# Two pools for the small tiles, and the start of every large SBUF tile moved to a multiple of 512 bytes

## The chip, the cores and the metric

The kernel runs on one core of a Trainium2 chip. The metric is the device time of one launch in microseconds. Three runs of the kernel before gave 735.39, 735.44 and 735.93 us, a median of 735.44 us.

## What is computed

Cut from the reference: an attention in both directions between `x` (8 batches, 8 heads, 512 tokens, depth 64) and `state` (32 rows for each head), and then a gated feed-forward layer on the 8 x (512 + 32) tokens of 512 numbers each.

```python
scores = scale * x @ state.T          # softmax over the 32 state rows
xread  = softmax(scores) @ state
scores2 = scale * state @ x.T         # softmax over the 512 tokens
sread  = softmax(scores2) @ x
x = concat([xread, sread]) as (4608 tokens, 512)
a = x @ w_a; b = x @ w_b              # 512 -> 1536
out = (a * b) @ w_out                 # 1536 -> 512
```

## The kernel before, in words

The 64-bit weights are split into a high and a low float32r part, and each product of the feed-forward layer is made of three TensorE matmuls (high by high, high by low, low by high).

The work goes by visits: a unit (one of the 8 batches, or `States`, the 256 state rows of all batches together) and a list of chunks of the 1536 hidden columns. Twelve column tiles `ft` of 128 make up the 1536. For each unit and `ft` there is a `layer1` and a `layer2`:

- `layer1` (batch): twelve 512-column matmuls into two PSUM banks `ab`. The weights loaded into TensorE (`lhsT`) are slices of `p_h` and `p_l`, the moving operand (`rhs`) is `at_h` or `at_l`.
- `layer2` (batch): twelve 512-column matmuls into four PSUM banks `acc`. The weights are slices of `g_h` and `g_l`, the moving operand is a half of a tile `wo0` to `wo11`.
- `layer1` of `States`: twenty-four 256-column matmuls, with weights from `wq` or `sw_st` and `x_nat` (high) or `x_raw` (low) as the moving operand.
- `project`: products of the states with the first weights, in pairs into a bank `ms` (the first ones into `acc`), with weights `sd_h`, `sd_l` and `wq` as the moving operand.

In every one of them each matmul has its own weight load. The three parts repeat in the order high-high, high-low, low-high.

All instructions are recorded first; then `plan` puts them in an order for each engine by costs and due times that are written in the kernel, and this order is issued as it stands (all of it from line 1047, which is why the profile shows that line alone). `plan` knows shapes, pool names as keys and numbers of buffers; it knows no addresses. All DMAs are issued from one queue (SP).

The small tiles are `m1` (three times 16 floats, 192 bytes in each partition, 2 buffers) and `m2` (4 floats, 16 bytes, 8 buffers of 32 bytes each with the padding); both hold the maxima and sums of the softmaxes. Before, both are tiles of the pool `att`.

The pools lie in SBUF one behind the other in the order in which they are opened. In the program of the kernel before, the first free byte of a partition is 16512, which is 128 more than a multiple of 512. The places that follow from it:

| tiles | first byte in the partition | remainder by 512 |
|---|---|---|
| `ident` (const0), `xst` (const) | 16512, 17024 | 128 |
| all of `proj`: `raw`, `t1`, `t2`, `wq`, `sd_h`, `sd_l`, `sw_st`, `wo0` to `wo11` | 21120 to 127616 | 128 |
| `x_raw` (first of att) | 127616 | 128 |
| `m1`, 2 buffers | 132224 | (small) |
| `s_p`, `x_nat`, `at_h`, `at_l` (att) | 132608 to 165376 | 0 |
| `m2`, 8 buffers | 165376 | (small) |
| `e2`, `a2`, `a_tr` (att) | 165632 to 171776 | 256 |
| all of `mlp`: `stg`, `p_raw`, `p_h`, `p_l`, `a_sb`, `g_h`, `g_l` | 171776 to 229120 | 256 |

Each large tile has a size that is a multiple of 512 bytes, and so has each slice that a 512-column matmul reads (128 columns of weights are 512 bytes, 512 columns are 2048).

Of the kernel before, what the change touches and what calls it, by code (L numbers as in the profile page):

```python
# [10 lines left out]
F32 = mybir.dt.float32  # L11
# [9 lines left out]
P = 128  # L21
# [393 lines left out]
def attn_moe(ctx, tc, xt, xn, sd, wl, w_out, out):  # L415
# [9 lines left out]
    def pool(name, bufs, free=False, **kw):  # L425
        p = Pool(ctx.enter_context(tc.tile_pool(name=name, bufs=bufs, **kw)), name, bufs, free)
        pools.append(p)
        return p

    const0 = ctx.enter_context(tc.tile_pool(name="const0", bufs=1))  # L430
    const = pool("const", 1)
    proj = pool("proj", 2)
    att = pool("att", 2)
    mlp = pool("mlp", 2)
    dram = pool("dram", 1, space=bass.MemoryType.DRAM)
    ps_acc = pool("ps_acc", 4, space=bass.MemoryType.PSUM)
    ps_ab = pool("ps_ab", 2, space=bass.MemoryType.PSUM)
# [5 lines left out]
    def minus(eng, out, in0, in1):  # L443
        eng.tensor_tensor(out=out, in0=in0, in1=in1, op=ALU.subtract)
# [149 lines left out]
    class Attention:  # L594
# [37 lines left out]

        def soft_t(self):

            m1 = self.m1 = att.tile([P, 3, 16], F32, name="m1")
            sp = self.sp
            t = self.t.rearrange("p (a b) -> p a b", b=32)
            nc.vector.tensor_reduce(out=m1[:, 0, :], in_=t, axis=AX.X, op=ALU.max)
            minus(nc.vector, sp, t, m1[:, 0, :].unsqueeze(2).broadcast_to([P, 16, 32]))
# [9 lines left out]

        def soft(self):  # L650

            m2 = self.m2 = att.tile([P, 4], F32, name="m2", bufs=8)
            nc.vector.tensor_reduce(out=m2[:, 0:1], in_=self.s, axis=AX.X, op=ALU.max)
            nc.vector.tensor_scalar_mul(out=m2[:, 1:2], in0=m2[:, 0:1], scalar1=-SCALE)
            if self.b not in WIDE:
                self.turn()
            nc.scalar.activation(out=self.e2, in_=self.s, func=AF.Exp, bias=m2[:, 1:2], scale=SCALE,
                                 accum_out=m2[:, 2:3])

        def turn(self):  # L660
            sp = self.sp
            nc.vector.transpose(out=sp.rearrange("p a b -> p (a b)"), in_=self.s)

            m1 = self.m1 = att.tile([P, 3, 16], F32, name="m1")
            nc.vector.tensor_reduce(out=m1[:, 0, :], in_=sp, axis=AX.X, op=ALU.max)
            minus(nc.vector, sp, sp, m1[:, 0, :].unsqueeze(2).broadcast_to([P, 16, 32]))

# [422 lines left out]
```

## Time and profile before

| | us |
|---|---|
| median of three runs | 735.44 |
| the profiled execution, its own time | 734.27 |
| its span, first to last instruction | 732.5 |
| TensorE matmuls busy | 706.2 |
| VectorE (DVE) busy | 495.8 |
| ScalarE (ACT) busy | 394.9 |

The span is the time from the first to the last instruction of the program; 1.8 us of the execution's time lie outside it. "PE" is TensorE's matmuls and "PEld" its weight loads, which overlap them. A matmul's own duration in the profile (about 0.4 us) is longer than the time from its start to the start of the next one, since matmuls are pipelined; what a row of matmuls costs is therefore read from starts, or from the chain of work that ended last, where each piece counts only the time that it adds.

### The profile page before, as it was taken

To read this page: it belongs to the slowest core of one execution; us is meant where nothing else is said; L and a number is where in the kernel's file an instruction comes from. 1 tells how busy PE (TensorE), PEld (TensorE's weight loads), DVE (VectorE), ACT (ScalarE), POOL (GpSimd) and SP (SyncE) were. 2 spreads that over 40 slices of the span, in tenths; PEclk is the share of its full clock that TensorE was granted. 3 is DMA by queue.
4 is the path that set the end of the run, shared out by engine and by line. 5 is a ranking of instruction groups with operands and counts; after the bars stand their busy time and mean duration, and the time that the engine had idled before them with its cause. 6 is when DMAs were issued, how large, how long until landed. Compare 5 with 4: busy or idle time off the path is not lost.

```text
span 732.5 us, 9629 instructions
## 1 busy us (share of the span) xinstructions
PE 706.2 (96%) x3440; PEld 557.7 (76%) x3440; DVE 495.8 (68%) x947; ACT 394.9 (54%) x723; POOL 0.7 (0%) x6
## 2 busy tenths in 40 slices
PE   5898899998999999999999999999999999999997
PEld 4565657785887888788888887886788888988886
DVE  5986795995847967684799548637879833795322
ACT  4966785686846459786445325234456433553222
POOL 0000000000000000000000000000000000000000
PEclk9999999999999999999999999999999999999999
DMA  9667867677788436859988133324425311501002
GB/s 339 219 225 276 278 238 241 240 278 268 259 286 309 158 142 243 272 193 354 356 314 288 38 115 123 115 64 134 159 57 198 119 58 30 199 31 30 1 0 87
DMA packets 55087, 134.32 MB, mean 183 GB/s; under 512 B 5632, under 2 KB 5632, under 8 KB 55040
## 3 DMA queue, kind: packets, MB, share of 16 engines
q1 hardware_dynamic: 55040, 133.71, 52.5%
q8 instruction: 27, 0.44, 0.3%
q14 instruction: 20, 0.16, 0.1%
HBM read 87.03 MB, written 46.66 MB: 183 GB/s over the span
## 4 chain that ended last, share of the span: by engine, by line
PE 92%; ACT 5%; DMA 1%; DVE 1%; issue 1%; DVEq 0%; SPq 0%; ACTq 0%
PE ab L1047 40%; PE acc L1047 39%; PE ms L1047 13%; ACT wq L1047 2%; DMA p_raw<-scr 1%; DMA x_raw<-xt 0%; ACT stg L1047 0%; ACT t L1047 0%; ACT wo L1047 0%; ACT p_h L1047 0%; ACT sd_h L1047 0%; ACT e L1047 0%; DVE m L1047 0%; ACT sw_st L1047 0%; ACT at_h L1047 0%
## 5 line engine op out<-in xcount | busy, mean ns | idle before, releaser
L1047 PE MATMUL acc<-wo,g_h 128*128 128x512 f32 x816 | 259.3, 397 | 0.1
L1047 PEld LDWEIGHTS acc<-wo,g_h 128*128 128x128 f32 x816 | 151.4, 188 | 37.0 <-issue 2.3
L1047 DVE TENSOR_TENSOR a_sb<-ab,a_sb 128x512 f32<-128x512 f32 (+1 forms) x108 | 71.3, 661 | 138.9 <-PE ab L1047 131.8
L1047 PE MATMUL acc<-wo,g_l 128*128 128x512 f32 x408 | 159.3, 396 | 0.0
L1047 PE MATMUL ab<-at_h,p_h 128*128 128x512 f32 x384 | 152.4, 400 | 1.9 <-ACT p_h L1047 1.7
L1047 PE MATMUL ab<-at_l,p_h 128*128 128x512 f32 x384 | 152.2, 397 | 0.0
L1047 PE MATMUL ab<-at_h,p_l 128*128 128x512 f32 x384 | 150.8, 396 | 0.0
L1047 ACT COPY a_sb<-ab 128x512 f32<-128x512 f32 (+1 forms) x108 | 60.9, 564 | 150.7 <-PE ab L1047 149.6
L1047 ACT CAST g_h<-a_sb 128x512 fp32r<-128x512 f32 (+1 forms) x108 | 64.6, 598 | 53.2 <-DVE a_sb L1047 52.9
L1047 PEld LDWEIGHTS acc<-wo,g_l 128*128 128x128 f32 x408 | 76.5, 188 | 18.3 <-issue 1.0
L1047 PEld LDWEIGHTS ab<-at_h,p_h 128*128 128x128 f32 x384 | 73.0, 190 | 22.4 <-ACT p_h L1047 3.6
L1047 PEld LDWEIGHTS ab<-at_h,p_l 128*128 128x128 f32 x384 | 72.7, 189 | 20.1 <-issue 3.1
L1047 PEld LDWEIGHTS ab<-at_l,p_h 128*128 128x128 f32 x384 | 72.9, 190 | 17.0 <-issue 1.8
L1047 DVE TENSOR_TENSOR g_l<-a_sb,g_h 128x512 fp32r<-128x512 f32 (+1 forms) x108 | 70.8, 655 | 20.9 <-ACT g_h L1047 20.8
L1047 DVE TENSOR_TENSOR p_l<-p_raw,p_h 128x512 fp32r<-128x512 f32 x92 | 60.0, 684 | 11.7 <-ACT p_h L1047 11.7
L1047 ACT CAST p_h<-p_raw 128x512 fp32r<-128x512 f32 x92 | 52.8, 619 | 13.8 <-PE ab L1047 9.3
L1047 DVE TENSOR_SCALAR t<-t 128x512 int32<-128x512 int32 x120 | 49.8, 422 | 9.6 <-ACT t L1047 8.5
L1047 PE MATMUL ms<-wq,sd_h 128*128 128x512 f32 (+2 forms) x112 | 38.8, 418 | 7.3 <-ACT wo L1047 3.9
L1047 ACT CAST wq<-t 64x512 fp32r<-64x512 f32 (+1 forms) x64 | 39.4, 619 | 8.2 <-PE ms L1047 2.9
L1047 DVE SCALAR_TENSOR_TENSOR t<-raw,t 128x512 int32<-128x512 int32 (+1 forms) x60 | 39.7, 686 | 0.3
L1047 PE MATMUL ms<-wq,sd_l 128*128 128x512 f32 (+2 forms) x112 | 37.7, 406 | 0.0
L1047 ACT COPY wo<-ms 128x512 f32<-128x512 f32 x44 | 25.8, 590 | 12.8 <-PE ms L1047 11.5
(93 smaller groups left out, 702.2 us busy)
## 6 DMA issues: line engine op xcount, KB each, us to landing
p_raw<-scr SPq DMA_DIRECT2D x46, 512.0 KB, 4.4
scr<-sw_st SPq DMA_DIRECT2D x48, 256.0 KB, 4.2
scr<-wo SPq DMA_DIRECT2D x48, 256.0 KB, 4.2
raw<-wl SPq DMA_DIRECT2D x22, 512.0 KB, 5.8
part<-stg SPq DMA_DIRECT2D x20, 512.0 KB, 3.0
stg<-part SPq DMA_DIRECT2D x20, 512.0 KB, 6.1
out<-stg SPq DMA_DIRECT2D x34, 256.0 KB, 2.4
x_raw<-xt SPq DMA_DIRECT2D x14, 576.0 KB, 3.9
```

The costliest lines, as they stand in the source:

```text
L1047: getattr(obj, method)(*map(real, args), **{k: real(x) for k, x in kw.items()})
```

## The change

A pool `small` is opened ahead of all others and holds the two buffers of `m1` (384 bytes), and a pool `tail` is opened behind `mlp` and holds the eight buffers of `m2` (256 bytes). No instruction is added, removed or given another shape, and no tile has another number of buffers.

```diff
+    small = pool("small", 2)
     const0 = ctx.enter_context(tc.tile_pool(name="const0", bufs=1))
     const = pool("const", 1)
     proj = pool("proj", 2)
     att = pool("att", 2)
     mlp = pool("mlp", 2)
+    tail = pool("tail", 8)
...
-            m1 = self.m1 = att.tile([P, 3, 16], F32, name="m1")
+            m1 = self.m1 = small.tile([P, 3, 16], F32, name="m1")
...
-            m2 = self.m2 = att.tile([P, 4], F32, name="m2", bufs=8)
+            m2 = self.m2 = tail.tile([P, 4], F32, name="m2")
...
-            m1 = self.m1 = att.tile([P, 3, 16], F32, name="m1")
+            m1 = self.m1 = small.tile([P, 3, 16], F32, name="m1")
```

The places follow from the sizes: 16512 + 384 = 16896 = 33 x 512, so `ident`, `xst`, all of `proj` and `x_raw` move up by 384 bytes to remainder 0; `s_p` to `at_l` stay where they were; `e2`, `a2`, `a_tr` and all of `mlp` move down by 256 bytes, also to remainder 0.

## Rows read from the trace of the kernel before

**Rows 1.** The page: busy time of each engine, granted clock, DMA share in 40 slices.
```profile
PE 706.2 (96%) x3440; PEld 557.7 (76%) x3440; DVE 495.8 (68%) x947; ACT 394.9 (54%) x723; POOL 0.7 (0%) x6
...
PEclk9999999999999999999999999999999999999999
DMA  9667867677788436859988133324425311501002
```

**Rows 2.** The page: the chain that ended last, by engine, as shares of the span.
```profile
PE 92%; ACT 5%; DMA 1%; DVE 1%; issue 1%; DVEq 0%; SPq 0%; ACTq 0%
```

**Rows 3.** Groups of matmuls by shape: count, busy us and mean ns, idle before.
```profile
L1047 PE MATMUL acc<-wo,g_h 128*128 128x512 f32 x816 | 259.3, 397 | 0.1
L1047 PE MATMUL acc<-wo,g_l 128*128 128x512 f32 x408 | 159.3, 396 | 0.0
L1047 PE MATMUL ab<-at_h,p_h 128*128 128x512 f32 x384 | 152.4, 400 | 1.9 <-ACT p_h L1047 1.7
...
L1047 PE MATMUL ms<-wq,sd_h 128*128 128x512 f32 x80 | 31.9, 399 | 3.1 <-ACT wo L1047 2.4 <-ACT sw_st L1047 0.8
```

**Rows 4.** The chain in order of time: start us, us added, engine and tile.
```profile
211.40 2.77 PE ab L1047 x12
...
267.12 0.93 PE ms L1047 x4
...
376.76 2.73 PE ab L1047 x12
379.50 2.79 PE acc L1047 x12
...
628.46 2.83 PE ab L1047 x24
...
700.53 2.73 PE ab L1047 x12
703.26 2.79 PE acc L1047 x12
```

**Rows 5.** TensorE's timeline, 203.1 to 204.5 us: start, duration, operation.
```profile
203.36 0.39 PE L1047 MATMUL ms<-wq,sd_h 128*128 128x512 f32 x1
203.59 0.39 PE L1047 MATMUL ms<-wq,sd_l 128*128 128x512 f32 x1
203.82 0.39 PE L1047 MATMUL ms<-wq,sd_h 128*128 128x512 f32 x1
204.04 0.40 PE L1047 MATMUL ms<-wq,sd_l 128*128 128x512 f32 x1
204.28 0.39 PE L1047 MATMUL ab<-at_l,p_h 128*128 128x512 f32 x1
```

**Rows 6.** Groups by shape again: DVE and ACT on tiles of different remainders, `States` matmuls.
```profile
L1047 DVE TENSOR_TENSOR p_l<-p_raw,p_h 128x512 fp32r<-128x512 f32 x92 | 60.0, 684 | 11.7 <-ACT p_h L1047 11.7
...
L1047 ACT CAST p_h<-p_raw 128x512 fp32r<-128x512 f32 x92 | 52.8, 619 | 13.8 <-PE ab L1047 9.3 <-DMA p_raw<-scr 4.3
...
L1047 DVE SCALAR_TENSOR_TENSOR t<-raw,t 128x512 int32<-128x512 int32 x30 | 20.6, 686 | 0.2
...
L1047 ACT CAST wq<-t 128x512 fp32r<-128x512 f32 x16 | 9.9, 622 | 2.6 <-PE ab L1047 2.0 <-DVE t L1047 0.6
...
L1047 DVE TENSOR_TENSOR at_l<-a_tr,at_h 128x512 fp32r<-128x512 f32 x12 | 8.2, 683 | 0.0
...
L1047 ACT CAST at_h<-a_tr 128x512 fp32r<-128x512 f32 x12 | 7.5, 621 | 5.4 <-DVE a_tr L1047 5.4
```

**Rows 7.** TensorE's busy time on `acc` in two stretches: length, busy (count), clock, DMA share, GB/s.
```profile
0.00:200.00 200.00, 64.55 (x274) 0.99 0.74 262
200.00:732.50 532.50, 257.84 (x1020) 1.00 0.45 154
```

**Rows 8.** DMA issues: source and target, count, KB each, median us to landing.
```profile
scr<-sw_st SPq DMA_DIRECT2D x48, 256.0 KB, 4.2
```

**Rows 9.** TensorE's waits: who waited for whom, us in total, times, longest.
```profile
PE ms L1047 <- DMA x_raw<-xt: 4.3, 1, 4.3
```

## The prediction

> **What bounds the kernel now.** I read the page first. [...] Next come the matmuls by shape: 1224 `acc` matmuls of `layer2` (816 + 408), 1152 `ab` matmuls of `layer1` (three groups of 384, of which one stands), and 160 `ms` matmuls of `project` (two groups of 80, one stands) [rows 3]. The mean ns there is no cost, because matmuls overlap; all of these groups show 396 to 400.
>
> The cost is in the chain in order of time. In the regular stretches (about 345 to 437, 565 to 622 and 650 to 705 us) it alternates between twelve `ab` matmuls in 2.73 us and twelve `acc` matmuls in 2.79 us [rows 4]. That is 227.5 against 232.5 ns for one. Both have 512 columns, 128x128 weights, their own weight load and the same clock. So an `acc` matmul costs 5 ns more for a reason that isn't its shape. The reader is to see that the pair of numbers is the same at 376 and at 700 us, where the DMAs are busy to eight tenths and to one tenth or less [rows 1, 4]: transfers don't explain it.
>
> What differs is where the operands lie. `acc` reads `wo` (remainder 128 by 512) against weights `g_h`, `g_l` (remainder 256): the two starts differ by 128 bytes modulo 256. `ab` reads `at_h`, `at_l` (remainder 0) against `p_h`, `p_l` (remainder 256): no difference modulo 256. The third kind, `ms`, reads `wq` (128) against `sd_h`, `sd_l` (128): no difference either. If the relation of the two operands sets the pace, `ms` must be able to run like `ab`. Between its first and its last start of the four at 203.36 lie 0.68 us, and the step from the third to the fourth is 0.22 us [rows 5]: three steps of 227 ns on the average, the pace of `ab` and not that of `acc` (three steps of `acc` would be 0.70). Longer runs of `ms` don't exist, and other groups of four take 0.93 us, 232.5 each [rows 4], so this is a hint and no proof. A hint too is that 128 bytes off a multiple of 512 is no fault in itself here, since both operands of `ms` are.
>
> **The change part by part.** No instruction and no wait is added or removed. Counts of buffers stay, and the planner sees no addresses, so the order on each engine should stay as well: nothing is moved past a queue. What is left is the new starts.
>
> *DVE and ACT: nothing.* The same kind of operation takes the same time at each remainder: subtraction 684 ns on `p_l`, `p_raw`, `p_h` (all 256) and 683 on `at_l`, `at_h` (0) with `a_tr` (256); cast 619 ns from 256 to 256, 621 from 256 to 0, 622 in `proj` (128); a two-input DVE operation on `t` and `raw` (128) 686 [rows 6]. Bound both ways: 3 ns of some 680, on engines with 32% and 46% of the span idle.
>
> *`m1`, `m2`: nothing.* Their operations have the same shapes at new places, still whole multiples of their element.
>
> *DMAs: nothing to gain that shows.* TensorE waits for a DMA once, for 4.3 us, for the first load of all [rows 9]. A store from `sw_st` (128) of 256 KB lands after 4.2 us [rows 8]; 96 such stores (48 here, 48 from `wo`) run beside TensorE. Bound: if each were shorter by a tenth, 0.4 us, that would be hidden by the matmuls; if the 1% of the chain that is DMA, 7 us, shrank by that tenth, 0.7 us. I take 0.
> [...]
>
> *`acc` matmuls: the term that counts.* After the change `wo` and `g_h`, `g_l` all have remainder 0. If they take the pace of `ab`, each gains 232.5 - 227.5 = 5 ns. Nearly all lie behind 200 us, where TensorE is hardly ever idle: 1020 there [rows 7], 5.1 us. The 204 others (1224 - 1020) lie in the first 200 us, where chains through ACT and DMA take turns with TensorE; I take half of 204 x 5 ns, 0.5 us. Bounds: 0, and 1224 x 6 ns = 7.3 us if the pace goes a little below `ab`'s.
>
> *`ab` matmuls: a little.* Outside the regular stretches a group of twelve takes 2.75 to 2.77 us instead of 2.73 [rows 4]; these groups come behind `ms` or broken `acc` groups, as if the pace needed some matmuls to settle after a change of operands. With all operands related alike there is less to settle: 0.02 to 0.04 us for about a third of 96 groups, 0.6 to 1.3 us; I take 0.6. Bounds: 1.3 us gained, and lost 1152 x 5 ns = 5.8 us if the new relation (0 against 0, before 0 against 256) is the worse one.
>
> *`ms` matmuls:* 160 x up to 5 ns = 0.8 us; half of it, 0.4.
>
> *`States` matmuls:* 24 of 256 columns take 2.83 us [rows 4], 118 ns each, more than half of 227.5 (114). 288 of them by 4 ns would be 1.2 us. A third of them (`x_raw`) has operands related like `ms`, two thirds (`x_nat`) like `acc`, and they aren't told apart by their group. I take 0, and keep 1.2 us as a bound.
>
> The sum: 5.1 + 0.5 + 0.6 + 0.4 = 6.6 us. The profiled execution took 734.27 us, so it would take 727.7; it lies 1.2 us below the median of the runs, 735.44, from which I get **728.8 us**. All gains at their bounds, 7.3 + 1.3 + 0.8 + 1.2 = 10.6, give 724.8.
>
> **The rivals.**
>
> *The addresses don't matter (no change, 735.4 us).* Then `acc` is slower for something else that `ab` doesn't have: it goes to a new PSUM bank every three matmuls, `ab` every six. For it: DVE and ACT show no trace of alignment [rows 6], and `x_raw` and `x_nat` have different remainders inside one group of `States`. Against it: `ms` changes its bank every two matmuls, and yet kept 227 ns for three steps [rows 5].
> [...]
>
> *The 256 bytes between the operands are what makes `ab` fast (slower, about 739.5 us).* After the change both operands begin at remainder 0. If weight load and moving operand get in each other's way when they start at the same remainder, `ab` goes from 2.73 to 2.79 us a group, and `acc` keeps its 2.79. Two thirds of the `ab` groups are at 2.73: 768 x 5 ns = 3.8 us, and some settling more: 735.4 + 4.1 = 739.5. It decides as soon as a regular `ab` group reads 2.79. For it: most `ms` groups, which have the same remainder in both operands, stand at 232.5 [rows 4]. Against it: [rows 5].
>
> *The DMAs become faster and that shows:* at most 0.7 us by the bound above, within what can't be told from no change; I count it there.
>
> **How the numbers follow.** A faster pace of `acc` by the relation of its operands: 0.58. Addresses without effect: 0.26. Same remainder worse: 0.13. Something else that costs, such as a changed order: 0.03. A measurement of this kernel can tell about 0.2% (1.5 us) from no change. Of the first case nearly all lies beyond that, 0.57; the second is nearly all within it; the last two are slower, 0.15 with a small share that stays within. So faster 0.57, same 0.28, slower 0.15. The range goes from 725.0 (the gains near their bounds) up to 737.0 (no change and 0.2%): it leaves out the slower cases and a little at the lower end, less than 2 in 10. The likeliest case's own range is 725.0 to 733.0, the upper end being less than half of the `acc` term.
>
> **What would show it.** Right: in the regular stretches `acc` x12 at 2.73 us or below, `ab` x12 still at 2.73 or a little below; durations on DVE and ACT unchanged; the same order on each engine; the waits of other engines for TensorE shorter. Wrong: `acc` x12 still at 2.79 (addresses without effect), or `ab` x12 at 2.79 as well (same remainder worse). It would be wrong in size if the time that TensorE saves comes back as idle time ahead of it, in waits for ACT or for loads, which now stand at a few us in all.

## The result, and the profile after

The changed kernel takes 727.24 us (median of 6 runs, 726.53 to 729.0) against 735.54 us (6 runs): a ratio of 0.9884, with a 95% interval from 0.9861 to 0.9907. The forecast was 728.8 us, with a range from 725.0 to 737.0. The profiled execution took 728.81 us with a span of 727.0.

The chain in order of time of the kernel after, against [rows 4]:

```profile
212.75 2.72 PE ab L1049 x12
...
267.70 0.91 PE ms L1049 x4
...
374.99 2.72 PE ab L1049 x12
377.71 2.72 PE acc L1049 x12
...
623.87 2.87 PE ab L1049 x24
626.75 2.75 PE acc L1049 x12
...
695.13 2.72 PE ab L1049 x12
697.85 2.72 PE acc L1049 x12
```

Twelve `acc` matmuls went from 2.79 to 2.72 us, 5.8 ns for each; twelve `ab` in a regular stretch from 2.73 to 2.72; an `ab` group behind `ms` and broken groups from 2.77 to 2.72; four `ms` from 0.93 to 0.91. In the regular stretches and around groups of `ms`, all 512-column matmuls now run at one pace, 2.72 / 12 = 226.7 ns, from the first one on. Beside the 256-column groups of `States` they don't: twelve `acc` matmuls there take 2.75 us. And one kind became slower: twenty-four 256-column matmuls of `States` mostly take 2.87 us, where they took 2.83.

TensorE's timeline of the kernel after, around the four `ms` matmuls of [rows 5]:

```profile
204.88 0.39 PE L1049 MATMUL ms<-wq,sd_h 128*128 128x512 f32 x1
205.11 0.39 PE L1049 MATMUL ms<-wq,sd_l 128*128 128x512 f32 x1
205.34 0.39 PE L1049 MATMUL ms<-wq,sd_h 128*128 128x512 f32 x1
205.56 0.39 PE L1049 MATMUL ms<-wq,sd_l 128*128 128x512 f32 x1
205.79 0.39 PE L1049 MATMUL ab<-at_l,p_h 128*128 128x512 f32 x1
```

From the first start to that of the `ab` matmul behind them are 0.91 us; before, 0.92. That last step, at the border between two kinds, was 0.24 us, and is 0.23.

What the prediction took for a settling of the pace is a price paid at such borders. In the kernel before, the first three steps from start to start inside a regular `ab` group that follows an `acc` group average 231.7, 232.5 and 230.8 ns (35 such groups in the trace), and the other nine 226.7 each, which is already the pace of the changed kernel. In the changed kernel all twelve are between 226.6 and 226.8. A border has its price without `acc`, too. Four `ms` matmuls between `ab` groups, first before the change and then after it:

```profile
268.74 1.39 PE ab L1047 x6
270.13 0.93 PE ms L1047 x4
271.06 1.37 PE ab L1047 x6
```

```profile
269.29 1.36 PE ab L1049 x6
270.65 0.91 PE ms L1049 x4
271.56 1.36 PE ab L1049 x6
```

Both kinds were well related to their own weights before. The starts of one kind against those of the other differed by 128 bytes modulo 256, and no longer do.

Groups by shape on the other engines after, against [rows 6]:

```profile
L1049 DVE TENSOR_TENSOR p_l<-p_raw,p_h 128x512 fp32r<-128x512 f32 x92 | 60.0, 684 | 12.5 <-ACT p_h L1049 12.5
...
L1049 ACT CAST wq<-t 128x512 fp32r<-128x512 f32 x16 | 9.9, 623 | 2.7 <-PE ab L1049 2.0 <-DVE t L1049 0.7
```

684 and 623 ns, before 684 and 622. On TensorE, DVE and ACT the operations stand in the same order as before, 3440, 947 and 723 of them. So no work was added or moved on these engines; what changed is TensorE's pace.

**Where the profiled execution shows less.** It is 5.5 us shorter in span (732.5 to 727.0), the medians 8.3 apart. The same `acc` group begins at 199.80 us before and at 201.42 after, and the same `ab` group at 340.84 and at 339.63. So the profiled changed kernel is 1.6 us behind at 200 us, and from there to its end it gains 7.1 us. Busy time and granted clock in the first two stretches, the kernel before and then the kernel after:

```profile
0.00:50.00 50.00, 38.94 (x217) 28.79 (x218) 38.04 (x76) 34.65 (x63) 0.70 (x6) 1.00 0.71 258
50.00:100.00 50.00, 42.30 (x240) 27.61 (x243) 38.77 (x86) 37.10 (x71) 0.00 (x0) 1.00 0.77 273
```

```profile
0.00:50.00 50.00, 37.06 (x212) 27.61 (x213) 36.62 (x73) 34.35 (x62) 0.70 (x6) 0.97 0.67 248
50.00:100.00 50.00, 42.80 (x229) 28.43 (x228) 36.88 (x82) 34.02 (x66) 0.00 (x0) 0.93 0.78 269
```

The columns are length, busy us (count) of PE, PEld, DVE, ACT and POOL, granted clock, DMA share and GB/s. The clock after was 0.97 and 0.93 of full speed there, 1.00 before. Read in windows of 0.2 us, it stood at 0.50 for one stretch of 3.4 us in the first 50 us and for two in the second, and at 1.00 outside them; the kernel before has none before 182 us. TensorE was busy for about as long in both executions (39 and 42 us before, 37 and 43 after), so what lowered the clock in one of them isn't shown. It differs between executions of one and the same kernel. The six runs of the changed kernel have mean clocks of 0.990, 0.995, 0.991, 0.995, 0.992 and 0.995 and take 728.81, 726.53, 727.84, 726.63, 729.0 and 726.64 us. From 340 us on, with the granted clock at 1.00 in both, the traces can be compared directly: to the first `ab` x24 of the last visit it takes 706.05 - 340.84 = 365.21 us before and 700.57 - 339.63 = 360.94 after, 4.3 us less in half of the kernel, and nothing is given back there.

Since the order is the same, the 7.1 us can be added up matmul by matmul from the starts: 5.1 on `acc`, 1.6 on `ab`, 0.5 on `ms` and 0.2 on others, less 0.4 lost on `States`.

### The profile page after: what moved, and what is told of

Same layout as the page of the kernel before. It is cut to its first block, busy times and chain, and to the rows that moved or that the text cites. A ratio compares the mean times of both kernels' runs of the same rounds, so it can differ in the third digit from the quotient of the medians.

```text
span 727.0 us, 9629 instructions
## 1 busy us (share of the span) xinstructions
PE 699.6 (96%) x3440; PEld 559.9 (77%) x3440; DVE 495.3 (68%) x947; ACT 395.1 (54%) x723; POOL 0.7 (0%) x6
## 4 chain that ended last, share of the span: by engine, by line
PE 91%; ACT 4%; DVE 3%; DMA 1%; issue 1%; SPq 0%; DVEq 0%; ACTq 0%
PE ab L1049 40%; PE acc L1049 38%; PE ms L1049 12%; ACT wq L1049 2%; DMA stg<-xt 1%; DVE t L1049 1%; DVE m L1049 1%; DVE s_p L1049 0%; ACT t L1049 0%; DVE p_l L1049 0%; ACT sd_h L1049 0%; SPq L1049 0%; ACT stg L1049 0%; ACT sw_st L1049 0%; ACT at_h L1049 0%
## 5 line engine op out<-in xcount | busy, mean ns | idle before, releaser
L1049 PE MATMUL acc<-wo,g_h 128*128 128x512 f32 x816 | 255.9, 393 | 0.2 <-DVE wo L1049 0.2
L1049 PE MATMUL acc<-wo,g_l 128*128 128x512 f32 x408 | 157.4, 392 | 0.0
```

The source lines that it names most:

```text
L1049: getattr(obj, method)(*map(real, args), **{k: real(x) for k, x in kw.items()})
```

## The experiments

The experiments set the forecast's theory, that the relation of the two starts modulo 256 bytes sets the pace, against its rivals and one more: every start has to be a multiple of 256 or 512 by itself. All experiments are the changed kernel with other places for the same tiles; none leaves out work. The gaps are a small unused tile, which GpSimd clears at the start:

```diff
+    def gap(name, size):
+        t = ctx.enter_context(tc.tile_pool(name=name, bufs=1)).tile([P, size // 4], F32, name=name)
+        base.gpsimd.memset(t, 0.0)
```

**1. All tiles at remainder 128** (against the changed kernel):

```diff
     small = pool("small", 2)
+    gap("gap", 128)
     const0 = ctx.enter_context(tc.tile_pool(name="const0", bufs=1))
```

> All large tiles begin at remainder 128 by 512, so no operand is at a multiple of 512 or 256, but the two operands of every matmul are related as in the changed kernel (difference 0). If the relation sets the pace: acc x12 and ab x12 at 2.72 us, 726.5 to 728.5 us in all, like the changed kernel. If each start has to be a multiple of 256 or 512: acc and ab x12 at 2.79 us, 736 to 741 us.

Measured: 727.33 us, ratio 0.9907 (0.9881 to 0.9934) to the kernel before (734.27 in these runs). Its chain:

```profile
605.62 2.72 PE ab L1054 x12
608.34 2.72 PE acc L1054 x12
...
622.12 2.87 PE ab L1054 x24
624.99 2.75 PE acc L1054 x12
```

No large tile begins at a multiple of 256, and the kernel is as fast as the changed one. The words "every large tile at a multiple of 512" describe what the change does; they aren't why it helps. It also settles the DMAs: loads and stores at 128 off a multiple of 256 do no harm to the kernel's time that can be measured (727.33 us, and 727.24 for the changed kernel). A 256 KB store from `sw_st` lands after 4.2 us here, 4.1 in the changed kernel and 4.2 before [rows 8]; one from `wo` after 4.0, 4.2 and 4.2.

**2. Only `m1` moved** (`proj` to 0, `mlp` stays at 256) **and only `m2` moved** (`proj` stays at 128, `mlp` to 0):

```diff
+    small = pool("small", 2)
...
-            m1 = self.m1 = att.tile([P, 3, 16], F32, name="m1")
+            m1 = self.m1 = small.tile([P, 3, 16], F32, name="m1")
...
-            m1 = self.m1 = att.tile([P, 3, 16], F32, name="m1")
+            m1 = self.m1 = small.tile([P, 3, 16], F32, name="m1")
```

```diff
+    tail = pool("tail", 8)
...
-            m2 = self.m2 = att.tile([P, 4], F32, name="m2", bufs=8)
+            m2 = self.m2 = tail.tile([P, 4], F32, name="m2")
```

These two diffs are against the kernel before.

> Only m1 is moved: proj at remainder 0, mlp stays at 256, so acc reads 0 against 256, ab 0 against 256 as before, ms 0 against 0. If the difference modulo 256 sets the pace: acc x12 at 2.72 to 2.74 us, 727 to 730 us in all. If multiples of 512 are needed: acc x12 stays near 2.79, 733 to 736 us. If the 256 bytes between the operands are what makes ab fast: acc as fast as ab and the whole faster than the changed kernel, 725 to 727 us.

> Only m2 is moved: proj stays at remainder 128, mlp goes to 0, so acc reads 128 against 0, ab 0 against 0, ms 128 against 128. If the difference modulo 256 sets the pace: acc x12 stays at 2.79 us, ab at 2.72 to 2.73, 733 to 735.5 us. If the weights' own start at a multiple of 512 is what counts: acc at 2.72, 727 to 729 us.

Measured: `m1` alone 727.1 us, ratio 0.9913 (0.9887 to 0.994); `m2` alone 735.76 us, ratio 1.0012 (0.9995 to 1.0029), 0.3 us above the range expected for it. The chains, first with `m1` moved and then with `m2`:

```profile
604.99 2.72 PE ab L1048 x12
607.71 2.72 PE acc L1048 x12
```

```profile
604.42 2.79 PE acc L1048 x12
607.21 2.73 PE ab L1048 x12
...
629.44 2.83 PE ab L1048 x24
```

The move of `m1` is the whole change; that of `m2` does nothing that can be measured. With `m1` moved `acc` reads 0 against 256 (2.72 us), with `m2` moved 128 against 0 (2.79 us), and before the change 128 against 256 (2.79 us). So a difference of 256 was as good here as none, 128 was bad from either side, and a multiple of 512 wasn't needed. `m2` moved leaves `ab` at 0 against 0 and at 2.73, not 2.72: its operands are fine, but it still pays at the border behind each `acc` group, as in the kernel before.

**3. A gap of 128 bytes ahead of `mlp`,** which makes `ab` bad too:

```diff
+    gap("gap", 128)
     mlp = pool("mlp", 2)
```

> The changed kernel with 128 bytes put between att and mlp: acc and ab both read remainder 0 against weights at 128; ms stays 0 against 0. If the relation sets the pace: acc x12 and ab x12 both at about 2.79 us, 1152 and 1224 matmuls by 5 to 6 ns more than in the changed kernel, 737 to 741 us. If only the moving operand's start counts, which is a multiple of 512 here: 2.72 for both, 726.5 to 729 us.

Measured: 739.69 us, ratio 1.0064 (1.0044 to 1.0083).

```profile
604.90 2.79 PE ab L1054 x12
607.70 2.79 PE acc L1054 x12
```

The same two tiles of `ab` that took 2.72 us take 2.79, with no other edit than 128 bytes ahead of the weights. With the addresses alone the kernel goes from 727 to 740 us: they aren't without effect on TensorE. And since the moving operands of both kinds begin at a multiple of 512 here, the moving operand's own start isn't what counts.

**4. Other gaps ahead of `mlp`,** 32 to 224 bytes, the edit as in 3. The gap of 64 has four runs, the others one each, since the chain shows the pace.

> As gap_128, with 64 bytes between att and mlp: acc and ab read remainder 0 against weights at 64. If only a multiple of 256 between the operands gives the quick pace: acc x12 and ab x12 at 2.77 to 2.79 us, 735 to 740 us. If the price grows with the distance up to 128: about 2.75, 731 to 735. If halves of 128 bytes count and 64 lies in the same half: 2.72, 726.5 to 729 us.

> As gap_128, with 32 bytes. Only multiples of 256: acc and ab x12 at 2.77 to 2.79 us. A price that grows with the distance: 2.73 to 2.74. Halves of 128 bytes: 2.72.

> As gap_128, with 192 bytes. Only multiples of 256: acc and ab x12 at 2.77 to 2.79 us. A price that grows with the distance to the nearest multiple of 256: as gap_64. Halves of 128 bytes: as gap_128, 2.79.

> The looks so far, for weights behind the moving operand by 0, 32, 64, 128, 192 and 256 bytes modulo 256: acc x12 at 2.72, 2.80, 2.80, 2.79, 2.75 and 2.72 us. If the pace falls off in steps of 32 bytes from 64 up: 2.79 to 2.80 for 96. If only the sides of 128 differ: 2.80.

> As gap_96, with 160 bytes. A slow descent from 128 to 256: 2.76 to 2.78 us for acc and ab x12. A step at 128: 2.75, as at 192.

> As gap_96, with 224 bytes. A slow descent to 256: 2.73 to 2.74 us for acc and ab x12. A step: 2.75, as at 192.

The chains for 32, 64, 96, 160, 192 and 224 bytes:

```profile
366.72 2.80 PE ab L1054 x12
369.52 2.80 PE acc L1054 x12
```

```profile
368.43 2.80 PE ab L1054 x12
371.23 2.80 PE acc L1054 x12
```

```profile
367.75 2.81 PE ab L1054 x12
370.57 2.81 PE acc L1054 x12
```

```profile
368.16 2.80 PE ab L1054 x12
370.96 2.80 PE acc L1054 x12
```

```profile
368.91 2.75 PE ab L1054 x12
371.66 2.75 PE acc L1054 x12
```

```profile
368.59 2.80 PE ab L1054 x12
371.39 2.80 PE acc L1054 x12
```

| weights' start minus moving operand's, modulo 256 | twelve 512-column matmuls, us | kernel, us |
|---|---|---|
| 0 (changed kernel, 1, `m1` moved) | 2.72 | 727 |
| 32 | 2.80 | 739.16 (one run) |
| 64 | 2.80 | 740.69 |
| 96 | 2.81 | 741.39 (one run) |
| 128 | 2.79 | 739.69 |
| 160 | 2.80 | 740.85 (one run) |
| 192 | 2.75 | 736.16 (one run) |
| 224 | 2.80 | 741.1 (one run) |

The gap of 64 has a ratio of 1.0082 (1.0067 to 1.0097) and lies just above its expected range. My three pictures for the shape (only multiples of 256, a price that grows with the distance, halves of 128 bytes) each had a number for 32, 64 and 192. Growth with the distance and halves are refuted by 32 bytes at the full price. "Only multiples of 256" holds but for 192 (the others took 2.79 to 2.81 us, where 2.77 to 2.79 were expected). 192 lies between, 2.5 ns a matmul above the best. After 192 there were two more pictures, a slow descent from 128 to 256 and a step at 128 (2.75 us from there on). Both are refuted by 160 and 224, at 2.80 us. In the kernel's time 192 (736.16 us) can't be told from the kernel before; only the chain sets it apart. Why 192 is better than its neighbours stays open.

**5. `x_nat` alone at 128 off,** to undo what the change did to `States`, with everything else as in the changed kernel:

```diff
     mlp = pool("mlp", 2)
+    gap("gap", 128)
+    xpool = pool("xpool", 1)
...
-                self.xn = att.tile([P, 4, 256], F32, name="x_nat", bufs=1)
+                self.xn = xpool.tile([P, 4, 256], F32, name="x_nat", bufs=1)
...
-            self.x = [att.tile([P, 4, B * NS], F32R, name=n, bufs=1) for n in ("x_nat", "x_raw")]
+            self.x = [p.tile([P, 4, B * NS], F32R, name=n, bufs=1) for p, n in ((xpool, "x_nat"), (att, "x_raw"))]
```

> The changed kernel with x_nat alone moved to remainder 128, behind mlp; the 256-column matmuls of States read it against weights at 0, as before the change. These groups went from 2.83 to 2.87 us with the change; if that too is the relation of the operands, the x24 groups are back at 2.83 while acc and ab x12 stay at 2.72, and the whole gains 12 x 0.04 = 0.5 us at most against the changed kernel, which the times won't tell: 726 to 728.5 us. If the 2.87 comes from something else, they stay at 2.87.

Measured: 726.84 us (724.88 to 729.59), ratio 0.9906 (0.9881 to 0.9931), not to be told from the changed kernel.

```profile
371.58 2.72 PE ab L1055 x12
374.31 2.72 PE acc L1055 x12
...
623.12 2.72 PE acc L1055 x12
625.85 2.84 PE ab L1055 x24
```

The 256-column groups are at 2.84 us, nearly where they were, and the 512-column ones stay at 2.72. So the place of `x_nat` is the cause there, with the sign turned round: these groups are a little better off with `x_nat` 128 bytes off, by 0.03 of 2.87 us. The twelve such groups are worth 0.4 us, less than the times can show. The `acc` groups behind them gain as well, from 2.75 to 2.72 us. Whether it is the distance of `x_nat` to the weights isn't shown: it also lies 128 bytes off `x_raw` now, which is the moving operand of every third matmul of these groups.

## Why the prediction was right

*The bound.* The sum counts the gain of `acc` behind 200 us in full. Right: TensorE holds the chain, 92% of the span before [rows 2] and 91% after, and what a matmul gained was paid nearly in full. From 340 us on nothing came back as idle time: TensorE is busy for all 360.00 us from 340 to 700, in both kernels.

*The reading that carried it.* Right. Shown by 1, 2 and 3: the pace of twelve 512-column matmuls follows the difference of the two starts modulo 256 (2.72 us at 0, 2.79 at 128) and neither start by itself. The hint from `ms` in [rows 5] pointed the right way. The groups of four `ms` at 0.93 us, which stood against it, are explained by the price of the border.

*The `acc` term.* Right: 5.1 us were forecast behind 200 us, and 5.1 are what the starts give there. That the two meet so closely is partly luck. In the regular groups an `acc` matmul gained 5.8 ns and not 5.0, since the 227.5 ns of `ab` had the slow steps behind the border in it; 1020 of those would be 5.9 us. Beside `States` `acc` gained less (six at 1.39 us before and after).

*The `ab` and `ms` terms.* Right in kind and undersized: `ab` gained 1.6 us behind 200 us alone, where 0.6 stood for all, and `ms` 0.5 there, where 0.4 stood for all. The settling vanished altogether, 15 ns for each regular group and up to 0.05 us for an irregular one (2.77 to 2.72).

*The sum.* 6.6 us were forecast, and the medians show 8.3. The traces give 7.1 from 200 us on. The other 1.2 lie in the first 200 us, where chains through ACT and DVE take turns with TensorE (which has 72% of the chain there before and 68% after), or in the scatter by the clock. The profiled executions can't tell these two apart, since their clocks differ there.

*`States`.* I took 0 with a bound of 1.2 us gained. They lost 0.04 us in most groups, 0.4 in all behind 200 us: a bound on the losing side was missing there.

*DVE, ACT, DMAs: nothing.* Right, by the groups after and by experiment 1. There all large tiles begin 128 off, and the kernel (727.33 us) shows no cost. Its stores' landings differ from the changed kernel's by 0.1 us upwards and 0.2 us downwards (4.2 and 4.0 us against 4.1 and 4.2), so they can't tell a cost of that size from none.

*The rivals.* Addresses without effect: refuted by 3, the same kernel at 740 us. The same remainder worse: refuted by `ab` at 2.72 with both at 0. Twelve matmuls with the same loads take 2.72 or 2.80 us, with 32 bytes between the tiles as the only difference. To agree with its own weights was not enough for a moving operand here: at the borders between `ab` and `ms`, each kind agreed with its own weights before, and six `ab` and four `ms` took 1.37 to 1.39 and 0.93 us, against 1.36 and 0.91 once both kinds began at the same remainder by 256. Which start of the neighbour counts, that of its weights or of its moving operand, no run here separates.

## What to carry to other kernels

When two groups of matmuls of one shape run at different paces in the chain, write down where their operands begin before looking for a scheduling reason. With float32r matmuls of 512 columns, each with its own weight load, put the weights and moving operands of all kinds that take turns at the same remainder by 256 bytes (here 2.72 us for twelve, against 2.75 to 2.81 at the seven other differences tried): small tiles with sizes that aren't multiples of 256 belong in a pool ahead of or behind all large ones, and here it was enough that the large ones agreed with each other (727.33 us with all of them at 128). A trace shows this without any new run if kinds with different relations stand side by side in it.

## What the runs showed of the hardware that I had not expected

- 32 bytes between the tiles cost as much as 128: 2.80 and 2.79 us against 2.72 for twelve matmuls, with an odd step at 192 (2.75).
- A border between kinds whose starts differ by 128 bytes has a price of its own: behind it the first three steps of an `ab` group took 231 to 233 ns and the other nine 226.7, though its own operands agreed. So the groups ran at 2.73 to 2.77 us, and at 2.72 once all starts agreed.
- The 256-column matmuls go the other way: 2.87 us for twenty-four with all operands at the same remainder, 2.83 or 2.84 with `x_nat` at 128 off.
- Executions of one kernel differ by several us, and the mean granted clock with them: with `m1` moved, 726.57 us at 0.995 and 731.91 at 0.988. In the profiled execution of the kernel before, the clock stood at 0.50 for one stretch of 3.4 us, and in that of the kernel after for four, all of them in the first 200 us; elsewhere it was 1.00.
